# Angle casts shared between VectorE and ScalarE, longer runs of idle products, and a new searched order in a fused attention and mixer kernel

## The chip, the core and the metric

The kernel runs on one core of a Trainium2 chip. The metric is the device time of one execution in microseconds (us). Executions of one kernel mostly lie within 1 to 2.5 us of each other here, so medians are quoted with their ranges. The runs after the first comparison were made in three sessions, each on another chip, and each session timed the kernel before again (medians 358.45, 358.45 and 358.40). A ratio is the mean time of one kernel's fast runs over that of the other's fast runs of the same rounds, so it is not quite the ratio of the medians that stand beside it. TensorE is the matrix engine, VectorE and ScalarE the two engines that empty its result memory (PSUM), GpSimd issues most loads.

## The reference, cut to what matters

```python
# attention with random features: batch 8, heads 8, 576 tokens, 64 channels, 128 features
proj = einsum('bhsd,md->bhsm', x, omega)
phi  = concatenate([cos(proj), sin(proj)], -1) / sqrt(128)        # for q and for k
kv, z = einsum('bhsm,bhsd->bhmd', k_p, v), sum(k_p, axis=2)
attn  = einsum('bhsm,bhmd->bhsd', q_p, kv) / einsum('bhsm,bhm->bhs', q_p, z)   # guarded
# mixer on x = attn with the heads side by side: (8, 576, 512)
u   = x + ((x^T @ U) @ V)^T                                        # rank 32
out = u + relu(u @ w_ch1) @ w_ch2                                  # 512 -> 2048 -> 512
```

## The kernel before

The work is cut into 1294 operations: for each of 32 head pairs (8 batches, 4 pairs each) the loads, transposes, angle products, casts, sines and cosines, the products with v, the numerator and the normalisation; for each batch the mixer's two dense layers. An angle comes out of TensorE in units of 1/65536 turn as fp32; it is cast to int32, and the low 16 bits, read as int16, are the angle modulo a turn. Sine reads them directly, cosine after a quarter turn is added.

```python
o_kc = add("kcp", "DVE", 1.14, rank, lambda _: nc.vector.tensor_copy(       # cast of the keys' angles
    i32(tt.t)[:, 1280:2304], kps.t.rearrange("p a b -> p (a b)")), ...)
...
def cang(...):  nc.vector.tensor_scalar(out=i32(cc.t)[:, 0:n], in0=tt.t[:, lo:lo+n, 0], scalar1=16384.0, op0=ALU.add)
def sin(...):   nc.scalar.activation(out=fe.t[:, 1, lo:hi], in_=tt.t[:, lo:hi, 0], func=ACT.Sin, scale=SIN_SCALE)
def cos(...):   nc.scalar.activation(out=fe.t[:, 0, lo:hi], in_=cc.t[:, 0:n, 0], func=ACT.Sin, scale=SIN_SCALE)
```

The order of the operations, the engine of those that may run on either, and the buffers are two constant tables that a search outside the kernel has found. `ORDER` is a list of operation numbers; a letter behind a number picks the first or second engine allowed. Each engine runs its own operations strictly in that order. While TensorE would wait in the first 36 us (by the kernel's own timetable), it is given products of a zero tile to keep its clock up:

```python
n = int((t - last - 0.3) / 0.1) if t < FILL else 0      # how many idle products fit before this operation
if n > 0 and f + 0.1 < last:
    fill(ps.t[b], n)                                    # n products zero x zero, 128 columns
```

Of the kernel before, what the change touches and what calls it, by code (L numbers as in the profile page):

```python
# [22 lines left out]
P = 128  # L23
# [96 lines left out]
20 22 49 0 7 21a 5 6 9 10 1 50 25 77 26a 23 27 78 29 53 28a 8 105 30 32 54b 33 31 36 3 55 57 35 37 4 51 34 174 56b  # L120
58 106 12 81 24 79 107 39 82b 201 52 175 60 2 38 59 18 61 173 16 40 62 229 63 83 64 84a 109 202 41 85 66 42b 65 88
87 90 86 67 257 69 111 68 230 19 80 89 70b 43 110a 91 44 71 11b 15 112b 72 92 114 117 108 13 113 94 116 73 93 97
95 258 96 120 115 98a 45 99 46b 119 118 176 121 74a 123 122 14 47 124 278 125 75 100 126a 101 277 48a 127 177 203
102a 339 128 179 231 76b 178b 103 180b 207 208b 205 104a 181 182 259 184 185 206b 1074 187 235 129 17 135 130b
236b 131 132b 183 186 209 138 139 212 136 188 233 189 137a 234b 145 146b 190 140a 211 1075 204 338 193 191 210 147
148a 261 192 214 163 164a 167 239 1073 262a 213 215 133 168b 159 263 281 194b 195 232 216 1076 160a 358 377 242
141 218 217 196 157 279 219 237 264a 221 238 142a 342 240 220 357 161 155 396 241 243 222b 162a 223 149 158b 464
244 134a 224 169 266 260 245 156b 150a 265 247 340 249 246 268 269 225 197 165 198b 226a 376 271 170a 361 153 199
248 482 267 250b 166a 251 154b 171 200b 273 272 151 152a 143 144a 270 252 172b 274 395 280 253 254b 282 359 328
1083 1084 283b 329 255 1085 330 275 276 332 1086 256b 341 334 284 227 463 501 285 1087b 380 1077 1078 228b 331 333  # L130
335 337 521 286 287a 343 348 350 288 336 360 1079 289b 1080 347 314 352 344a 316 349 378 351 1081b 315a 345 397
312 465 317b 304 346 313b 353 305b 310 399 362 354 311b 368 296 367 366 484 588 355 320 483 589 356 1095 379 398
297a 467 363b 364 371 466 290 607 1096 1082 1097 321b 369 502 291b 370 372 306 374 307a 365 381 373 375 318 1098
385 382b 383 386 319a 486 388 390 1099b 389 292 384 1100 627 302 1089 520 293a 387 391 303a 393 646 392 324 1088
400 325b 454 456 503 1090 1091 453 394 457 401b 458 522 455 485 322 323a 402 300 294 298 403 301b 295b 460 1092
459 468 299b 473 505 404 590 472 476 1093b 1113 475 469b 1114 713 1094 405b 1115 478 1116 477 474 479 481 410
1117a 411 413 406 407 308 412 1101 480 309a 1102 409 1103 408 487 326 461 1104 462 491 488a 492 493 495 327a 1105b
470 496 504 489 497 1107 609 471 490 523 1108 1109 494 506 1110 498 500 511 524 1111b 507b 425 426a 512 429 510
591 592 1119 515 608 1120 1112 414 1121 430b 514 516 645 1122 423 513 732 415 517 419 628 499 1123a 1106 519 424b
525 578 647 526a 420a 518 579 610 431 439 508 432a 582 416 752 440a 580 1118 584 527 451 452a 581 583 509 441 449  # L140
442a 427 445 450a 629 528 529 428a 530a 585 593 446a 600 435 436a 443 444a 447 598 715 437 599 611 714 597 605
594a 417 448a 531 601 539 540 602 532 626 1125 1126 421 630 1127 587 734 418b 541 438a 648 1128 535 586 422b 753
533 603 534 595 1129b 1131 1132 1133 1124 604 536 537 606 596 1134 1135 538 612 1143 616 617 620 618 622 621 619
623 1144 1145 613a 1146 550 772 551a 558 770 751 1147 559b 649 552 553b 562 631 624 717 632b 572 733 1136 625 563b
546 547a 635 614 839 638 858 433 716 636 637 573b 877 840 639 640 1137 615 1138 1139 1140 568 434b 771 1141 1130
736 641 642 650 569b 704 643 644 651a 703 1149 560 706 735 876 561a 633 707 705 634 708 652 755 709 548 574 544
549a 1150 710 575a 653 545a 774 554 718 724 555a 654 1151 1152 1148 576 655b 577a 556 754 723 722 725 730 660 838
1153 661 726 566 570 571b 557a 662 656 1161 711 719b 564 1162 657 727 664 665 567b 895 663 1163 773 728 659 1164
565a 1165 712 542 737 741 743 742 543a 1167 1168 720 658 859 1166 857 729 746 1142 1169 745 691 692a 666 738b 744
685 747 748 842 686a 749 1170 878 721 1171 841 693 964 695 696b 756 761 861 763 694a 683 757b 762 731 671 760 860  # L150
669 750 684b 764 739 672b 1155 1156 896 758 740 897 766 1157 699 767 681 765 670a 1158 700a 982 769 759 775 768
965 1159 682b 830 1173 697 1174 831 880 776b 698a 829 777 828 833 1175 1176 832 1160 778 687 835 834 1177 688b
1178 679 843 837 779 1001 680b 848 849 850 673 780b 1179 879 667 1172 844a 781 847 851 782 689 1154 899 789 854
690a 1180 785 675 674b 677 790 786 853 836 1002 845 846 668a 701 852 1181 1182 1183 676a 678a 702a 784 862 1197
866 867 1198 791 870 783 868 863a 855 856 869 787 871 1199 1200 826 873 872 827a 881 898 1201 963 983 885 984 888
886 874 788 808 967 1191 864 882b 1003 1192 1193 1194 889 890 891 887 893 812 806 809a 865 1195 900 875 813a 807b
1196 892 894 810 955 954 824 1215 1216 953 825a 957 883 966 901b 956 960 902 804 811a 884 805a 1202 814 815a 818
903 904 905a 819a 794 959 1217 985 906 907 795a 958 1218 822 968 1219 972 975 823a 969b 816 973 1203 817b 986 1204
820 910 1205 1005 908 976 961 1206 977 974 978 911 1220 909 798 821a 987 1207 1184 1185 799b 979 993 1004 796 797a
994 802 988a 962 991 792 1186 800 980 803a 1187 913 914 912 992 1188 1189 995 981 915 793a 970 801a 996 971 943  # L160
1209 997 1210 1211 1212 998 944a 1000 1213 1006 1007a 1011 1010 1014 1012 949 1013 950a 1221 1222 919 989 920b 947
917 990 999 918b 923 1016 1015 1008 948a 1017 1020 929 924b 1214 1018 916 933 1019 1190 1208 1021a 1022 1009 1023
939 934a 921 930a 940b 1223 1024 1224 1225 1226 937 1025b 1030 1031 1033 927 922a 1026 938b 945 1027 1034 1233 931
1234 946a 925 1235 926a 928b 1236 1237 941 942a 935 1032 936a 932b 1227 1228 1029 1028 1229 1230 1238 1059 1035
1055 1060b 1037 1231 1065 1036 1066b 1056a 1039 1038a 1251 1252 1253 1254 1255 951 952b 1061 1040b 1257 1258 1047
1051 1048a 1259 1071 1052a 1072a 1260 1062b 1256 1261 1045 1067 1239 1068a 1053 1054b 1046a 1240 1063 1049 1050a
1241 1232 1041 1269 1064b 1270 1271 1272 1042b 1242 1043 1243 1273 1262 1069 1245 1057 1244 1070b 1274 1044b 1246
1247 1248 1058a 1249 1263 1281 1282 1275 1264 1250 1265 1266 1267 1268 1276 1277 1278 1279 1283 1284 1280 1287
1288 1289 1285 1286 1290 1291 1292 1293
"""  # L170
SLOTS = """
001012000103011100001411023251001002010000110112113100010103021102010001020120001013002021101312001221000000201101
020131110010214512211101010200200102113011010012201200100110100011020210111101231030240100102221213011100122210013
011225103010001002101002010102121111202210120130200211021210120031121003010122000011001110103002031010212001200211
011004123101311002021250001201203011001320012102111011023200031002102011001001210100100101321001011201312102022001
211100201001301221001021000003100021100200401101021012102100001321112511030020112001100001221011002121013210021120
013211001032002101001011020220110011100201100102010123011010013211011021100012020100021101200011020130111012010213
12201100001320102010100220210221100100110111202110101200120020201112002010200001000122021201012021002
"""

LAT = {"PE": 0.21, "DVE": 0.14, "ACT": 0.16, "POOL": 0.2, "SP": 0.15}


class Plan:
    def __init__(self):
        self.ops = []

        self.rings, self.hw, self.landed = 0.0, 0.0, []

    def add(self, *a, **k):  # L190
        o = Op(*a, **k)
        self.ops.append(o)
        return o
# [170 lines left out]
    def emit(self, order, at, nc, fill, ps):  # L364
        left, free = {}, {}
        for o in order:
            for u in o.uses:
                left[u] = left.get(u, 0) + 1
        last = 1.2
        for o, t in zip(order, at):  # L370
            for u in o.uses:
                if u.t is None:
# [20 lines left out]
def kernel(  # L393
# [145 lines left out]
    def attention(g):  # L539
# [114 lines left out]
        def i32(t):  # L654
            return t.rearrange("p a c -> p (a c)").bitcast(I32)
# [377 lines left out]
```

## Time and profile before

| | before |
|---|---|
| time, first three executions | 358.57 us median (357.65 to 359.02) |
| TensorE busy | 346.0 us of 356.5, 4136 products, 90 of them idle ones |
| VectorE, ScalarE, GpSimd busy | 258.2, 211.3, 87.9 us |
| first sine on ScalarE starts | 8.22 us |
| numerator of head pair 3 (product 405) starts | 29.10 us |
| from there to the start of the last product | 322.57 us |

The last three rows split the span in the two pieces that the prediction works with. In that split "the head" is all before the numerator of the fourth head pair of batch 0, and "the dense part" all from it on. Of the groups of instructions, the large cast is the one that the change moves (columns: line, engine, operation, tiles, shapes, count, then busy us and mean ns, then idle time before it):

```profile
L657 DVE CAST tt<-pp 128x1024 int32<-128x1024 f32 x32 | 39.0, 1219 | 7.3 <-PE pp L620 7.1
```

These are the second five transposes of head pair 3, which need its q load (called q3 below):

```profile
17.83 0.45 PE L596 MATMUL pb<-ident,qk 128*128 128x128 bf16 x5
```

There is no bracket behind it: TensorE did not wait for q3, which the trace shows landing at 12.80 or 13.49 us (two q loads follow each other there).

### The profile page before, as it was taken

The page shows a single profiled execution, that of the slowest core. Times are in us where ns is not written, and L with a number is a line of the kernel's source. Part 1 is how long each engine was busy: PE and PEld are TensorE (multiplying, and loading weights), DVE is VectorE, ACT ScalarE, POOL GpSimd, SP SyncE. Part 2 cuts the span into 40 slices and gives each one's busy share as a digit, 9 for nine tenths or more (in the row PEclk, how much of TensorE's full clock was granted, in tenths as well). Part 3 has the DMA queues.
Part 4 walks back from the last instruction along what each step waited for, and adds up shares of the span by engine and source line. Part 5 has one row for each costly group of instructions (what it writes and reads, how often), then busy time and mean ns, then how long its engine had stood idle before and what let it go on. Part 6 is the DMA issues. An engine that isn't in the chain of part 4 may idle for free.

```text
span 356.5 us, 9601 instructions
## 1 busy us (share of the span) xinstructions
PE 346.0 (97%) x4136; PEld 190.9 (54%) x4136; DVE 258.2 (72%) x422; ACT 211.3 (59%) x274; POOL 87.9 (25%) x147
## 2 busy tenths in 40 slices
PE   7879999999999999999999999999999999999994
PEld 5666566555556454555545654665445644455442
DVE  4999997797988778698768989778876853232411
ACT  3998998869575778265575674875746722121000
POOL 8884635442231435041201313001000000000000
PEclk9999999999999999999999999999999999999999
DMA  8999999999949899799747729708320415021223
GB/s 137 179 193 208 173 199 153 146 167 150 131 79 128 146 146 132 116 167 100 109 83 152 119 48 168 123 8 121 71 49 2 98 32 95 0 61 31 60 60 88
DMA packets 67403, 39.45 MB, mean 111 GB/s; under 512 B 47264, under 2 KB 61600, under 8 KB 67360
## 3 DMA queue, kind: packets, MB, share of 16 engines
q0 software_dynamic: 17376, 18.36, 37.0%
q1 hardware_dynamic: 49904, 20.34, 34.1%
q8 instruction: 32, 0.52, 0.6%
q10 hardware_dynamic: 80, 0.13, 0.1%
q14 instruction: 11, 0.09, 0.1%
HBM read 37.11 MB, written 9.44 MB: 131 GB/s over the span
## 4 chain that ended last, share of the span: by engine, by line
PE 93%; ACT 5%; DMA 1%; issue 0%; DVE 0%; POOLq 0%
PE pb L919 35%; PE pb L865 31%; PE pp L705 5%; PE pb L884 4%; PE pp L720 4%; PE pp L620 2%; ACT f L689 2%; ACT f L686 2%; PE pp L832 2%; PE pb L634 1%; PE pb L596 1%; DMA qk<-in_q_dram 1%; PE pp L726 1%; PE pb L791 1%; PE pb L996 1%; PE pb L924 1%
## 5 line engine op out<-in xcount | busy, mean ns | idle before, releaser
L865 PE MATMUL pb<-uT,W1b 128*128 128x512 bf16 x512 | 123.2, 379 | 0.0
L919 PE MATMUL pb<-W2b,hid 128*128 128x512 bf16 x512 | 122.0, 379 | 0.0
L689 ACT ACTIVATE f<-cc 128x1152 bf16<-128x1152 int16 (+1 forms) x64 | 74.3, 1162 | 21.2 <-DVE cc L682 19.7
L812 ACT ACTIVATE hid<-pb 128x512 bf16<-128x512 f32 x81 | 47.6, 597 | 64.1 <-PE pb L865 64.0
L686 ACT ACTIVATE f<-tt 128x1152 bf16<-128x1152 int16 (+1 forms) x64 | 74.4, 1162 | 9.9 <-PE pp L726 3.4
L919 PEld LDWEIGHTS <-hid 128*128 128x128 bf16 x512 | 48.1, 98 | 56.0 <-issue 3.1
L865 PEld LDWEIGHTS <-W1b 128*128 128x128 bf16 x512 | 47.5, 98 | 55.7 <-issue 3.0
L682 DVE TENSOR_SCALAR cc<-tt 128x1152 int32<-128x1152 int16 (+1 forms) x64 | 52.2, 816 | 1.2
L953 DVE TENSOR_TENSOR o<-pb,x 128x512 f32<-128x512 f32 x24 | 16.5, 689 | 44.6 <-PE pb L919 44.1
L584 POOL COPY v<-vraw 128x576 bf16<-128x576 bf16 x32 | 24.0, 751 | 92.9 <-PE pp L705 49.5
L657 DVE CAST tt<-pp 128x1024 int32<-128x1024 f32 x32 | 39.0, 1219 | 7.3 <-PE pp L620 7.1
L810 DVE TENSOR_SCALAR hid<-pb 128x512 bf16<-128x512 f32 x47 | 31.8, 684 | 13.4 <-PE pb L865 13.2
L666 DVE CAST tt<-pb 128x512 int32<-128x512 f32 x48 | 32.1, 682 | 2.1 <-PE pb L634 1.9
L555 POOL DMA_DIRECT2D qk<-in_q_dram x32 | 19.6, 620 | 31.3 <-DMA qkt<-qk 20.9
L735 DVE TENSOR_TENSOR x<-pp,rc 128x640 bf16<-128x640 f32 x32 | 26.4, 825 | 1.1
L705 PEld LDWEIGHTS <-f 64*128 64x128 bf16 x1152 | 19.6, 94 | 10.7 <-issue 6.4
L705 PE MATMUL pp<-v,f 64*128 64x65 bf16 x1152 | 23.2, 190 | 0.9 <-ACT f L689 0.9
L837 DVE TENSOR_TENSOR x<-pp,x 128x1024 bf16<-128x1024 f32 (+1 forms) x18 | 18.7, 1043 | 6.9 <-PE pp L832 6.6
L555 POOL DMA_DIRECT2D qk<-in_k_dram x31 | 18.4, 595 | 20.3 <-DMA qkt<-qk 16.2
L720 PEld LDWEIGHTS <-f 128*128 128x128 bf16 x512 | 19.9, 98 | 5.7 <-ACT f L689 0.3
L720 PE MATMUL pp<-kvb,f 128*128 128x65 bf16 x512 | 21.4, 194 | 0.1
L583 POOL DMA_DIRECT2D vraw<-in_v_dram x32 | 18.8, 591 | 3.8 <-issue 2.4
(80 smaller groups left out, 300.9 us busy)
## 6 DMA issues: line engine op xcount, KB each, us to landing
out_dram<-o SPq DMA_DIRECT2D x71, 128.0 KB, 2.5
qk<-in_q_dram POOLq DMA_DIRECT2D x32, 144.0 KB, 5.7
vraw<-in_v_dram POOLq DMA_DIRECT2D x32, 144.0 KB, 6.0
qk<-in_k_dram POOLq DMA_DIRECT2D x31, 144.0 KB, 5.8
W1b<-in_moe_w_ch_dram POOLq DMA_DIRECT2D x2, 1024.0 KB, 12.9
W2b<-in_moe_w_ch_dram POOLq DMA_DIRECT2D x4, 512.0 KB, 11.1
uT<-x SPq DMA_TRANSPOSE x30, 2.6
qkt<-qk SPq DMA_TRANSPOSE x24, 6.4
```

The lines of the kernel that those rows point to most:

```text
L555: nc.gpsimd.dma_start(qk.t[:, lo:lo + NJ, :], src[b, 2 * hp:2 * hp + 2].rearrange("h (p j) d -> (h p) j d", j=NJ))
L657: o_kc = add("kcp", "DVE", 1.14, rank, lambda _: nc.vector.tensor_copy(i32(tt.t)[:, 1280:2304], kps.t.rearrange("p a b -> p (a b)")), deps ...
L666: nc.vector.tensor_copy(i32(tt.t)[:, 640 * lo:640 * lo + 512], t.t)
L682: nc.vector.tensor_scalar(out=i32(cc.t)[:, 0:n], in0=tt.t[:, lo:lo + n, 0], scalar1=16384.0, scalar2=None, op0=ALU.add)
L686: nc.scalar.activation(out=fe.t[:, 1, lo:hi], in_=tt.t[:, lo:hi, 0], func=ACT.Sin, scale=SIN_SCALE)
L689: nc.scalar.activation(out=fe.t[:, 0, lo:hi], in_=cc.t[:, 0:n, 0], func=ACT.Sin, scale=SIN_SCALE)
L705: nc.tensor.matmul(kvp.t[:, hh, 65 * s:65 * s + 65], fe.t[pr, s, 1152 + P * jj:1280 + P * jj], v65.t[pr, KJ[jj], :], start=(jj == 0), stop ...
L720: nc.tensor.matmul(nps.t[:, hh, 65 * i:65 * i + 65], fe.t[:, s, c0:c0 + 128], kvb.t[:, hh, s, :], start=(s == 0), stop=(s == 1))
L810: nc.vector.tensor_scalar(out=o, in0=i, scalar1=0.0, scalar2=None, op0=ALU.max)
L812: nc.scalar.activation(out=o, in_=i, func=ACT.Relu)
L865: nc.tensor.matmul(hp_.t, w1h[:, ct, fs], uT.t[:, ct, 0:512], start=(ct == 0), stop=(ct == NCT - 1))
L919: nc.tensor.matmul(d, w, W2b[c4][:, f % 4, :], start=(f == 0), stop=(f == NFT - 1))
```

## The change

The intent is to let the search place each angle cast on either engine, to fill TensorE's holes in the head more tightly, and to use a new order found with more slack for late transfers.

```diff
-    o_om = add("om", "SP", 0.43, ..., post=1.35)
+    o_om = add("om", "SP", 0.43, ..., post=1.8)
...
-        last = 1.2
+        last = 1.0
...
-                n = int((t - last - 0.3) / 0.1) if t < FILL else 0
+                n = int((t - last - 0.15) / 0.107) if t < FILL else 0
...
+        both = ("DVE", "ACT")
-        o_kc = add("kcp", "DVE", 1.14, rank, lambda _: nc.vector.tensor_copy(
-            i32(tt.t)[:, 1280:2304], kps.t.rearrange("p a b -> p (a b)")), ...)
+        o_kc = add("kcp", both, (1.14, act(1024)), rank, lambda e: copy(
+            e, i32(tt.t)[:, 1280:2304], kps.t.rearrange("p a b -> p (a b)")), ...)
... (the same for tcp, 256 columns, and qcp, 512 or 1024 columns)
-ORDER, SLOTS = ... (1294 places)
+ORDER, SLOTS = ... (another order of the same 1294, 54 of 120 casts on ScalarE)
```

Part of the order of the loads (V is the mixer's small matrix, q3 the q load of head pair 3):

```diff
 old, loads in order:  ... k3  v1  q4  q3  V  v2  v3 ...
 new, loads in order:  ... v0  k3  k4  V  q3  v1  v2  v3 ...
```

## The prediction

> **What bounds the kernel now.** I read the page first (its shares and its chain), then the busy time by stretches, then the timeline of TensorE and of ScalarE in the first 30 us.
>
> ```profile
> PE 346.0 (97%) x4136; PEld 190.9 (54%) x4136; DVE 258.2 (72%) x422; ACT 211.3 (59%) x274; POOL 87.9 (25%) x147
> ...
> PE 93%; ACT 5%; DMA 1%; issue 0%; DVE 0%; POOLq 0%
> ```
>
> TensorE is busy for 97% of the span and is 93% of the chain that ended last; ScalarE has 5%. VectorE, whose casts the change moves, has none. A mean does not say where the last 3% lie, so I cut the span:
>
> ```profile
> 13.00:20.00 7.00, 5.97 (x164) 5.13 (x162) 6.96 (x11) 6.95 (x12) 6.17 (x11) 1.00 1.11 173
> 20.00:24.00 4.00, 2.76 (x70) 2.09 (x68) 3.90 (x8) 3.98 (x5) 3.61 (x7) 1.00 1.14 202
> 24.00:29.00 5.00, 3.62 (x83) 2.56 (x82) 4.93 (x11) 5.00 (x7) 3.40 (x6) 1.00 1.17 209
> ...
> 32.00:60.00 28.00, 28.00 (x447) 16.47 (x445) 26.43 (x42) 27.03 (x40) 14.32 (x21) 1.00 1.24 182
> 60.00:340.00 280.00, 280.00 (x3175) 149.19 (x3174) 202.73 (x325) 159.64 (x203) 49.45 (x80) 1.00 0.65 98
> ```
>
> The columns after the stretch's length are busy us of TensorE, its weight loads, VectorE, ScalarE, GpSimd. From 13 to 29 us it is the other way round from the rest: VectorE and ScalarE are full (ScalarE 15.93 of 16 us, VectorE 15.79), while TensorE has holes. From 32 us on TensorE has not one hole. The border is in TensorE's timeline:
>
> ```profile
> 28.73 0.24 PE L791 MATMUL pb<-x,Ub 128*32 128x128 bf16 x4 [0.36 <-DVE x L735]
> 28.79 0.22 PE L793 MATMUL pb<-x,Ut 128*32 128x128 bf16 x1
> 29.10 0.68 PE L720 MATMUL pp<-kvb,f 128*128 128x65 bf16 x16
> 29.62 0.29 PE L726 MATMUL pp<-kvb,f 128*128 128x65 bf16 x4
> ```
>
> L720 at 29.10 is the numerator of the fourth head pair of batch 0; it needs that pair's last cosine. Before it stand waits in brackets; after it no start is later than the columns of the matmul before it explain, but for about 95 ns at each change of tile shape. So the kernel is two pieces in series: a head to 29.10 us, paced by ScalarE and VectorE, and a dense TensorE part to the last product's start at 351.67. What does not shorten the head or the dense part's own work is worth nothing. The head's last steps on ScalarE are these:
>
> ```profile
> 12.47 0.58 ACT L806 COPY qkt<-pb 128x512 bf16<-128x512 bf16 x1 [0.49 <-PE pb L596]
> 12.95 1.27 ACT L689 ACTIVATE f<-cc 128x1280 bf16<-128x1280 int16 x1
> ...
> 26.84 1.15 ACT L686 ACTIVATE f<-tt 128x1152 bf16<-128x1152 int16 x1
> 27.89 1.15 ACT L689 ACTIVATE f<-cc 128x1152 bf16<-128x1152 int16 x1
> ```
>
> From the first sine at 8.22 to the last cosine's end at 29.04 ScalarE waits once, 0.49 us. One 1152-column sine starts 1.06 us after the last.
>
> **What the Trainium skill says.** "ScalarE: Activation LUTs", section "What ACT_TABLE_LOAD costs": an activation costs 186 ns + 0.833 ns per column, and neighbours overlap by about 93 ns. The trace agrees: 597 ns for 512 columns of L812 (the page's 613), 1162 for 1152 (1146). The same page, "Table sets: the hidden batching unit", has copy and relu in every set; the trace shows one table load of 1.28 us among sines, copies and relus, so a cast on ScalarE adds no load. "VectorE: DVE Perf Modes", section "Why PSUM operands drop a tier": fp32 from PSUM runs at one element a cycle; the 1024-column cast's 1219 ns is in line with 0.96 GHz plus overhead. "TensorE: Matmul & The Clock Gate", section "What's actually happening": half clock until about 3.4 us of sustained activity in a free-running window. The trace has 128-column products 106 ns apart up to about 12.0 us and 56 ns after it.
>
> **The change, part by part.**
>
> *Casts.* By the built programs, 54 of 120 angle casts move to ScalarE: 12 of the 32 1024-column key casts, 2 of 8 query casts of 1024, 27 of 48 of 512, and 13 of 32 tails of 256. Against them 16 `hid` relus of 512 go from ScalarE to VectorE (63 for 47), besides smaller copies. A 1024-column cast holds VectorE 1.14 us (start to start, 6.97 to 8.11); on ScalarE I estimate 0.92 (the 1024-column sines are 0.95 apart). In the dense part neither engine is the bound: VectorE loses 27 x 0.60 + 14 x 1.14 + 13 x 0.33 = 36 us there and in the head and gains about 10 of relus, and that buys nothing by itself.
>
> *The head, replayed by hand.* I took the new order of each engine and gave each instruction the start-to-start time that it has in the old trace. First, the input side. The first q load lands at 5.41 in both (it is first on its queue); TensorE transposes it in order at 5.46, five cold products and two idle ones, and the key angles start near 6.2 and end near 6.85, as before. The keys' first transposes do come 0.3 us earlier, since the cast no longer stands behind omega's, but they only wait for q then. Now ScalarE casts the keys (6.9 to 7.85) and the tail (to 8.12), instead of VectorE, and the first sine starts at 8.12 (8.22 before). From there ScalarE has:
> - batch 0's sixteen sines and cosines: 2 x 0.95 + 2 x 1.17 + 12 x 1.06 = 16.96 us, unchanged;
> - one query cast of 1024 (0.92), two tails (0.54), one kvb copy (0.26), the U casts (0.68), one hu copy (0.15): 2.55 us. The old order has there three qkt copies, two kvb, U and hu: 0.58 + 0.48 + 0.70 + 0.52 + 0.68 + 0.15 = 3.11 us, and the 0.49 us wait.
>
> Sum: 8.12 + 16.96 + 2.55 = 27.63, against 28.94 (start of the next operation in the old trace). VectorE keeps up in the replay, with 19.2 us of work from 6.05 on (7 transposed-tile copies, 5 of 8 large casts, 8 additions of a quarter turn at 0.68 to 0.88, two normalisations of 1.18, the small copies): its last addition would end at 26.2 and is needed at 26.56. So the gain is about 1.3 us, with only 0.3 us of margin on VectorE. I take back 0.3 us for waits that such a replay misses (the old order had 0.49). Head: -1.0 us.
>
> *Idle products.* There are 90 before and 90 after; only their places change: 27 in place of 19 at the start, more but shorter groups later. All lie before L720's place, where 405 products stand in both orders, and the useful ones among them have the same counts line by line. So they neither lengthen nor shorten the dense part. Could they warm the clock earlier? The first group ends near 3.87 instead of 3.0 and the hole after it shrinks from 0.9 to about 0.25 us, but TensorE still stops for q before 5.46. If that counts as idle, the warm clock comes at about 9 to 12 us as before. It would be worth up to 0.5 us if it came at 5. Mean: -0.1.
>
> *The dense part.* From product 405 on both have 3731 products of the same counts. Tile shapes change 76 times for 77: -0.1 us. The tail (4.4 us from the last product's end, fin and two stores) has the same instructions; -0.0.
>
> *Later loads.* W1's first half is now the 22nd load on its queue instead of 14th. Loads land 0.71 us apart in the old trace, a half of W1 takes 5.2 to 5.8. I estimate 28.3 us for the first half (first used near 32), 35 for the second (near 40), and 38 to 51 for the four parts of W2 (first used near 55, the last near 60). No wait, but less margin on W1 than before (24.41 for 32.28).
>
> Sum: 358.57 - 1.0 - 0.1 - 0.1 = 357.37; I say 357.3 us, 0.4% less.
>
> **Rivals.** (1) *VectorE takes the bound in the head*: with ScalarE relieved, a 0.2 us slip of several additions (they vary from 0.67 to 0.90) delays the last cosine. For it: VectorE was 15.79 of 16 us busy. Against: the new order takes two and a half large casts off it there. Then nothing is gained: 358.4. (2) *The dense part gets holes*: 16 more relus on VectorE, casts waiting behind sines on ScalarE, W1 later by 4 us. For it: from 32 to 60 us both engines are 94% and 97% busy. Against: the first W2 product comes earlier (place 823 for 896), which thins their work there. Cost 0.5 to 2 us: 358 to 359.5. (3) *The clock warms in the first 5 us*: everything before 9 us shortens, the first sine starts near 7.6: 356.6. (4) *The casts count in full*: 36 us off VectorE shorten the span by per cents. VectorE's 0% of the chain speaks against it; I give it nothing.
>
> **Range and chances.** The terms that can move are the head (-2.0 to 0) and holes (0 to +1.2); runs of before alone lie from 357.65 to 359.02. So 356.0 to 358.5 should hold it 8 times in 10. Two per cent is 7.2 us, half of the 15 us in which the head does no useful product at all, and far beyond either term: faster 0.01, same 0.98, slower 0.01.
>
> **What would show it.** Right: ScalarE's first sine near 8.1, its last cosine of batch 0 ending near 27.7, the L722 numerator at product 405 near 27.8 to 28.1, TensorE full from there on, clock warm at 9 to 12 us, the casts on ScalarE near 1.04 us each. Wrong: a bracketed TensorE wait after 30 us (rival 2), ScalarE's sines waiting for `cc` between 13 and 27 us (rival 1), 56 ns spacing before 8 us (rival 3). The prediction fails as a whole if the dense part's length from product 405 to the last product differs from 322.6 us by more than 0.5.

## The result, and the profile after

| | before | changed |
|---|---|---|
| median of the first four executions | 358.45 us (357.65 to 359.02) | 358.01 us (357.93 to 358.41) |
| ratio | | 0.9992, 95% interval 0.9971 to 1.0013 |
| head (numerator starts) | 29.10 | 28.53 |
| dense part | 322.57 | 322.79 |
| span of the trace | 356.5 | 356.2 |

The outcome is "same", inside the predicted range, 0.7 us above the predicted 357.3. Six more executions in a later session gave 357.61 (356.89 to 358.40; ratio 0.9957, interval 0.9916 to 0.9998, widened by the two slow executions of before). Without those two the means of that session differ by 0.8 us. All ten together have a median of 357.94. So there is probably a gain, of about half a microsecond, but the first comparison alone does not show it: its interval holds 1.

The page of the changed kernel, its line of busy times and its chain by engine:

```profile
PE 345.7 (97%) x4136; PEld 191.0 (54%) x4136; DVE 237.1 (67%) x398; ACT 226.3 (64%) x298; POOL 84.3 (24%) x147
...
PE 89%; ACT 2%; DMA 2%; DVE 2%; POOL 2%; issue 1%; ACTq 0%; DVEq 0%; POOLq 0%
```

VectorE lost 21.1 us of work (the counts of the prediction had about 26) and ScalarE gained 15.0; TensorE has the same. In the chain VectorE and GpSimd now appear with 2% each, and DMA has 2% instead of 1%: something in the head waited for a load. The busy times by stretches (columns as in the prediction):

```profile
13.00:20.00 7.00, 5.35 (x114) 4.50 (x106) 5.61 (x10) 5.44 (x10) 4.69 (x11) 0.76 0.97 156
...
24.00:29.00 5.00, 4.08 (x101) 3.15 (x100) 4.88 (x11) 4.95 (x7) 1.91 (x3) 1.00 1.06 180
...
32.00:60.00 28.00, 27.94 (x422) 16.33 (x420) 25.14 (x43) 25.00 (x34) 13.59 (x22) 1.00 1.23 183
60.00:340.00 280.00, 280.00 (x3205) 149.32 (x3198) 183.87 (x297) 175.84 (x233) 48.75 (x83) 1.00 0.59 99
```

From 32 us on it is the same picture as before: TensorE without a hole worth naming. But from 13 to 20 us, where ScalarE had been full (6.95 of 7 us), it is busy for 5.44, VectorE for 5.61, and the granted clock of TensorE is 0.76. TensorE's timeline tells what happened:

```profile
13.61 0.39 PE L635 MATMUL pp<-qkt,WT 64*128 64x512 bf16 x2
15.53 0.71 PE L597 MATMUL pb<-ident,qk 128*128 128x128 bf16 x5 [1.53 <-DMA qk<-in_q_dram]
16.04 0.85 PE L998 MATMUL pb<-zero 128*128 128x128 bf16 x6
16.68 1.09 PE L722 MATMUL pp<-kvb,f 128*128 128x65 bf16 x16
...
18.23 0.28 PE L627 MATMUL pp<-qkt,WT 64*128 64x128 bf16 x1
...
28.53 0.68 PE L722 MATMUL pp<-kvb,f 128*128 128x65 bf16 x16 [0.39 <-ACT f L691]
```

TensorE stood 1.53 us for q3 (L597 is the line of the transposes), and what follows runs at half clock: sixteen numerator products take 1.09 us, against 0.68 for sixteen such products at 28.53. The chain of the first 35 us, followed back, gives the load its length (start, us, what): it was issued at 7.40 and landed 8.08 us later, at 15.48.

```profile
7.40 8.08 DMA qk<-in_q_dram
```

ScalarE's timeline shows the two ends of this story:

```profile
7.07 1.07 ACT L688 ACTIVATE f<-tt 128x1024 bf16<-128x1024 int16 x1
...
18.57 0.37 ACT L808 CAST tt<-pp 128x256 int32<-128x256 f32 x1 [1.51 <-PE pp L628]
...
27.32 1.16 ACT L691 ACTIVATE f<-cc 128x1152 bf16<-128x1152 int16 x1
```

The first sine starts at 7.07, a full microsecond before the predicted 8.12. TensorE's clock was already warm at 5.1 us, and the first q load landed at 4.83, where the kernel before had it at 5.41; the runs below tell the two apart. Then ScalarE waits 1.51 us for the tail angles of head pair 2, which TensorE computed at 18.23 (L627 and L628). This wait is the only one of its kind, and it took back all of the early start and more. Two theories were open: q3's late landing costs the time whatever the clock does, or the clock's relapse after the wait costs it.

### The profile page after: what moved, and what is told of

Read it like the earlier page. It is cut to its first block, busy times and chain, and to the rows that moved or that the text cites. A ratio compares the mean times of both kernels' runs of the same rounds, so it can differ in the third digit from the quotient of the medians.

```text
span 356.2 us, 9626 instructions
## 1 busy us (share of the span) xinstructions
PE 345.7 (97%) x4136; PEld 191.0 (54%) x4136; DVE 237.1 (67%) x398; ACT 226.3 (64%) x298; POOL 84.3 (24%) x147
## 4 chain that ended last, share of the span: by engine, by line
PE 89%; ACT 2%; DMA 2%; DVE 2%; POOL 2%; issue 1%; ACTq 0%; DVEq 0%; POOLq 0%
PE pb L921 35%; PE pb L867 30%; PE pp L707 5%; PE pp L722 4%; PE pb L886 4%; DMA qk<-in_q_dram 2%; PE pp L834 2%; PE pp L621 2%; PE pb L635 1%; ACT f L691 1%; PE pp L728 1%; POOL qk L556 1%; ACT f L688 1%; DVE tt L806 1%; PE pb L793 1%
## 5 line engine op out<-in xcount | busy, mean ns | idle before, releaser
L921 PE MATMUL pb<-W2b,hid 128*128 128x512 bf16 x512 | 123.9, 379 | 0.0
L688 ACT ACTIVATE f<-tt 128x1152 bf16<-128x1152 int16 (+1 forms) x64 | 73.6, 1162 | 11.0 <-PE pp L728 8.8
L814 ACT ACTIVATE hid<-pb 128x512 bf16<-128x512 f32 x64 | 37.3, 595 | 49.0 <-PE pb L867 48.8
L812 DVE TENSOR_SCALAR hid<-pb 128x512 bf16<-128x512 f32 x64 | 43.1, 685 | 20.0 <-PE pb L867 19.6
L684 DVE TENSOR_SCALAR cc<-tt 128x1152 int32<-128x1152 int16 (+1 forms) x64 | 49.9, 789 | 5.2 <-ACT tt L808 4.2
L806 DVE CAST tt<-pp 128x1024 int32<-128x1024 f32 (+1 forms) x45 | 38.9, 878 | 10.2 <-PE pp L621 5.6
L585 POOL COPY v<-vraw 128x576 bf16<-128x576 bf16 x32 | 22.4, 706 | 87.7 <-PE pp L707 38.1
L808 ACT CAST tt<-pp 128x1024 int32<-128x1024 f32 (+1 forms) x27 | 18.8, 704 | 8.9 <-PE pp L628 4.4
L722 PEld LDWEIGHTS <-f 128*128 128x128 bf16 x512 | 20.7, 99 | 6.9 <-ACT f L691 0.5
L806 DVE CAST tt<-pb 128x512 int32<-128x512 f32 x21 | 14.4, 687 | 10.8 <-PE pb L635 10.6
L808 ACT CAST tt<-pb 128x512 int32<-128x512 f32 x27 | 15.5, 586 | 8.2 <-PE pb L635 8.0
```

Of the source, the lines that this page charges most:

```text
L722: nc.tensor.matmul(nps.t[:, hh, 65 * i:65 * i + 65], fe.t[:, s, c0:c0 + 128], kvb.t[:, hh, s, :], start=(s == 0), stop=(s == 1))
L806: nc.vector.tensor_copy(o, i)
L808: nc.scalar.copy(o, i)
L812: nc.vector.tensor_scalar(out=o, in0=i, scalar1=0.0, scalar2=None, op0=ALU.max)
L814: nc.scalar.activation(out=o, in_=i, func=ACT.Relu)
L921: nc.tensor.matmul(d, w, W2b[c4][:, f % 4, :], start=(f == 0), stop=(f == NFT - 1))
```

## The experiments

Twelve runs were made. The edits of ORDER are shown as the words that move.

**V behind q3.** The load of V took from 11.94 to 14.86, and q3 stood behind it.

```diff
-... 57 12 106 81 51 ...      (12 is V, 106 is q3)
+... 57 106 12 81 51 ...
```

> The changed kernel with one load moved: V's broadcast is issued just behind the q load of the fourth head pair (q3) instead of just ahead of it. Theory: in the changed kernel q3 landed at 15.48 us because V ahead of it took 2.92 us, TensorE stood 1.53 us for it in order, and that came back as ScalarE's one wait of 1.51 us. Then q3 should land near 12.7, both waits vanish, the numerator at product 405 start at 27.0 to 27.5 instead of 28.53, and the kernel take 356.5 to 357.0. Rival (VectorE is next in line at once): numerator within 0.3 us of 28.53, 358.0. Rival (the head does not set the end): numerator earlier, but the last product no earlier than 351.3.

Measured: 356.73 us median (356.61 to 357.33), ratio to before 0.9961 (0.9948 to 0.9975). q3 landed at 13.30, TensorE's wait and ScalarE's 1.51 us were gone, and the numerator started at 27.25. But the dense part had 323.41 us, 0.6 more than in the changed kernel. TensorE's timeline:

```profile
27.25 0.67 PE L722 MATMUL pp<-kvb,f 128*128 128x65 bf16 x16
...
32.66 1.68 PE L867 MATMUL pb<-uT,W1b 128*128 128x512 bf16 x7 [0.62 <-DMA W1b<-in_moe_w_ch_dram]
```

With the head shorter, the next load was late: the first half of W1 landed at 32.61 (30.98 in the changed kernel), and half of the gain went there.

**q3 one place later.** If q3's landing sets the head's end, delaying it must cost.

```diff
-... 57 12 106 81 51 56a 38 ...
+... 57 12 81 51 106 56a 38 ...
```

> The changed kernel with the q3 load one place later still, behind a v load. Theory (q3's landing sets the end of the head): it lands near 16.2, TensorE's wait for it grows from 1.5 to about 2.2 us, the numerator starts near 29.2 and the kernel takes about 358.7. Rival (q3 hidden by something else): numerator still at 28.5, 358.0. Two idle products fewer stand in it by the kernel's own rule (88 for 90), which neither theory cares for.

Measured: 357.22 us (356.75 to 357.81), ratio 0.9972 (0.9955 to 0.9989). It was not slower but faster, so the theory as I had put it fell. The trace is a lucky control: V took only 1.75 us this time, q3 landed at 15.46, within 0.02 us of the changed kernel's first trace, and TensorE stood for it almost as long:

```profile
15.51 0.45 PE L597 MATMUL pb<-ident,qk 128*128 128x128 bf16 x5 [1.12 <-DMA qk<-in_q_dram]
...
15.91 0.68 PE L722 MATMUL pp<-kvb,f 128*128 128x65 bf16 x16
...
16.81 0.23 PE L627 MATMUL pp<-qkt,WT 64*128 64x128 bf16 x1
```

The clock stayed warm. From the transposes to L627 it took 1.30 us instead of 2.70 (15.53 to 18.23), ScalarE did not wait at all, and the numerator started at 27.16. The same landing with a warm and with a cold clock thus differs by 1.4 us at L627, of which 0.2 are four idle products fewer on the way: with all six, warm traces take 1.52 and 1.53 us (after_again, after_steady_fill). (Two of its idle products had moved into the wait, which shortened the stand from 1.5 to 1.1 us and may be why the clock held.)

**A short and a long start.** The changed kernel with 19 idle products at the start, and the kernel before with 27.

```diff
-n = int((t - last - 0.15) / 0.107) if t < FILL else 0
+n = (19 if last == 1.0 else int((t - last - 0.15) / 0.107)) if t < FILL else 0    # changed kernel
-n = int((t - last - 0.3) / 0.1) if t < FILL else 0
+n = (27 if last == 1.2 else int((t - last - 0.3) / 0.1)) if t < FILL else 0       # kernel before
```

> The changed kernel with 19 idle products at the very start, as before, in place of 27. Theory: the early warm clock (56 ns spacing from 4.9 us on) comes from the unbroken start; with 19 there is a hole of about 1 us and the clock warms at 8 to 12 us; the first sine starts near 8.1 instead of 7.07, but the numerator stays near 28.5 and the time near 358.0, since q3's landing sets them. Rival (the clock alone makes the changed kernel's small gain): numerator 1 us later, 359.0. Rival (phase of the clock's window is luck): warm before 5.5 us with 19 too.

Measured: 357.48 us (357.05 to 358.02), ratio 0.9979 (0.9963 to 0.9996). The clock warmed at 10.3 us, as expected, and the first sine started at 7.80. The numerator did not stay at 28.5, it came at 27.78: q3's landing at 15.69 still held TensorE for 0.87 us, but with the later start ScalarE did not wait. This run also parts the two causes of the early sine. Its first q load landed at 4.78, as in the changed kernel's first trace, and its sine is 0.7 us later: that is the start and its clock. The second trace below has a late clock too, but that load at 5.35, and its sine comes another 0.3 us later: that is the load.

> The kernel before with 27 idle products at the very start in place of 19. Theory: clock warm before 5.5 us, first sine near 7.3 instead of 8.22, and since ScalarE is full from there on the numerator at product 405 starts 0.5 to 1.0 us earlier than 29.10 and the kernel takes 357.5 to 358.0. Rival (loads set the head there too): first sine earlier, numerator within 0.2 us of 29.1, 358.4. Rival (phase is luck): clock still cold until 9 to 12 us.

Measured: 357.87 us (357.14 to 357.91), ratio 0.9987 (0.9973 to 1.0001), which is not clear of noise. In its trace the clock was warm at 4.6 us, the first sine at 7.13 and the numerator at 27.86. So the longer start probably helps the old order too, in an execution where it works; but this trace is the fastest of the five executions, and its first q load landed early (4.49).

**The changed kernel again**, for a second trace.

> The changed kernel unaltered, for a second trace and five more times. Theory (in the first trace the 1.5 us stand for q3 fell into one window of the clock gate, the clock went cold from 15.5 to 18.6 us, and ScalarE's 1.51 us wait came from that): if the clock stays warm in this trace, the numerator starts near 27.3 to 27.8 though q3 again lands near 15.5, ScalarE's wait is under 0.5 us and the profiled time is about 357.2; if it goes cold, 28.5 and 358.0 as before. Rival (q3's landing alone): numerator at 28.3 or later with a warm clock too.

Measured: 357.61 us (356.89 to 358.40). This time the clock warmed only at 10.2 us and had no relapse. TensorE's and ScalarE's timelines:

```profile
15.68 0.45 PE L597 MATMUL pb<-ident,qk 128*128 128x128 bf16 x5 [0.59 <-DMA qk<-in_q_dram]
...
28.00 0.68 PE L722 MATMUL pp<-kvb,f 128*128 128x65 bf16 x16
```

```profile
8.08 1.07 ACT L688 ACTIVATE f<-tt 128x1024 bf16<-128x1024 int16 x1
...
18.04 0.36 ACT L808 CAST tt<-pp 128x256 int32<-128x256 f32 x1
```

q3 landed at 15.63, as late as ever, and cost ScalarE nothing: the tail cast that had waited 1.51 us starts here at 18.04 with no bracket, because ScalarE, one microsecond later by its first sine, comes to it only then.

**Idle products in the wait for q3.** 24 of them ahead of the five transposes.

```diff
-n = int((t - last - 0.15) / 0.107) if t < FILL else 0
+n = (24 if o is self.ops[111] else int((t - last - 0.15) / 0.107)) if t < FILL else 0
```

> The changed kernel with 24 idle products ahead of the five transposes that stand for q3 (24 x 56 ns = 1.34 us, less than the 1.53 us wait). q3 lands as late as ever. Theory (cold clock after the wait is the cost): clock warm throughout from 5 us on, TensorE's wait there under 0.4 us, numerator near 27.3 to 27.8, median 357.2. Rival (q3's landing is the cost): numerator at 28.5, 358.0. If the idle products run late they may cost up to 0.3 us.

Measured: 357.77 us (357.22 to 358.52), ratio 0.9964 (0.992 to 1.0009). Inconclusive: the clock warmed at 10.2 us in this trace, so that there was nothing for the idle products to prevent. They ran until 16.5, 0.8 us past q3's landing at 15.75. The numerator came at 28.29.

**V behind q3 and W1 earlier.** The q load of pair 4 (174) and W1's first half (18) move forward.

```diff
-... 230 52 13 80 86 ... 278 120 174 46b ... 73 99 18 118a ...
+... 230 52 13 174 18 80 86 ... 278 120 46b ... 73 99 118a ...
```

> V behind q3 as in the run above, and besides the q load of pair 4 and W1's first half issued two loads earlier, ahead of the loads of pair 8. In the run with V behind q3 the first W1 product waited 0.62 us for W1, which landed at 32.61. Theory: W1 lands near 29 to 31, that wait goes, the dense part from the numerator on is 322.6 to 322.9 us for 323.4, and the kernel takes 356.1 to 356.4. Rival (another transfer then comes late, pair 8's or v's): the dense part stays at 323.3, 356.7.

Measured: 356.56 us (356.46 to 358.25), ratio 0.994 (0.9898 to 0.9982). W1 landed at 27.02 and its wait is gone. The profiled execution was the slowest of the six (358.25): the clock warmed at 10.3 us, the numerator started at 28.05, and the dense part had 323.55 us with other short waits, one of 0.27 us for VectorE. So in this trace the rival's longer dense part came, though TensorE shows no wait for another load in it. Four executions lay at 356.5 and two at 357.6 and 358.25.

**The head's casts back on VectorE.** Two casts of 1024 columns and three of 256, in the version with V behind q3, with the idle products held at their places.

```diff
-... 32b ... 33b ... 62b ... 89b ... 117b ...
+... 32a ... 33a ... 62a ... 89a ... 117a ...
```

> V behind q3, with the five casts of the first four head pairs that the change gave to ScalarE put back on VectorE (two of 1024 columns, three of 256), the same order and the same 90 idle products at the same places. Theory (in the head the casts matter, VectorE and ScalarE being full there): VectorE has 3.3 us more work and ScalarE 2.6 less; VectorE becomes the bound, ScalarE waits for cc 1.5 to 2.5 us in sum, the numerator starts 1.0 to 2.0 us later than 27.28, and the kernel takes 357.7 to 358.7. Rival (the casts are worth nothing, the start and the loads made the gain): numerator within 0.4 us of 27.3, 356.8.

Measured: 360.12 us (359.27 to 362.77), ratio 1.004 (0.9982 to 1.0097). ScalarE then waits for the casts and for the additions, for example:

```profile
14.91 2.22 ACT L688 ACTIVATE f<-tt 128x1152 bf16<-128x1152 int16 x2 [2.02 <-DVE tt L806]
19.98 1.16 ACT L691 ACTIVATE f<-cc 128x1152 bf16<-128x1152 int16 x1 [1.52 <-DVE cc L684]
```

The direction is as expected, the cost larger: about 3.4 us by the medians (360.12 less 356.73; different sessions). The profiled execution was the slowest (362.77). Its numerator started at 33.63, over 6 us later than with V behind q3 where 1 to 2 were expected, and its clock was cold from 15.6 to 19.0 and from 22.4 to 29.3 us, so its waits are not those of the casts alone. This version keeps an order made for the other placing, so it overstates what the casts alone are worth.

**The dense part's casts back on VectorE.** The other 49 casts, the same way, with the head as it is.

```diff
-words such as 184b 186b 240b ... (49 casts of head pairs 4 to 31)
+              184a 186a 240a ...
```

> V behind q3, with the 49 casts of the other 28 head pairs that the change gave to ScalarE put back on VectorE, order and 90 idle products as they are. Theory (in the dense part the casts' engine buys nothing while neither VectorE nor ScalarE is full): VectorE is busy about 268 us for 237, ScalarE about 190 for 226, the head is as in the run with V behind q3 (numerator 27.2 to 28.1), and the dense part is 323.4 us plus 0 to 1.0 for holes where an order made for ScalarE puts several casts in a row on VectorE; 356.7 to 358.0. Rival (the casts count in full): VectorE's 31 us more give a kernel longer by several us, over 360.

Measured: 373.23 us (372.85 to 374.40), ratio 1.0411 (1.0385 to 1.0438). My expectation was wrong by 15 us. The page's busy line, and the longest waits of TensorE by cause (us in total, times, longest):

```profile
PE 348.9 (94%) x4136; PEld 190.9 (51%) x4136; DVE 266.8 (72%) x447; ACT 198.6 (53%) x249; POOL 85.5 (23%) x147
```

```profile
PE pp L722 <- DVE tt L806: 1.9, 4, 1.0
PE pb L921 <- DVE tt L806: 1.9, 2, 1.5
```

The head was untouched (numerator at 27.27), and the dense part took 339.44 us. VectorE is busy for 72% of the span here, the very share that it had in the kernel before, where TensorE did not wait for it after 29.10, and yet TensorE now waits for it all along. The work is not quite equal (266.8 us for 258.2; the span is longer too), so the amount is not ruled out. But 8.6 us more in a dense part that is 16 us longer points to where the casts stand: with a cast too many in a row on an engine that keeps its order, the product behind it waits. No run gave this placing an order of its own.

**The kernel before again.**

> The kernel before, unaltered, for a second trace. Theory (the moment at which the clock warms is luck of its window, about 5 or about 10 to 12 us, and sets the spread within one kernel): from the first sine to the numerator again 20.7 to 20.9 us, dense part 322.6; the first sine lies at 7.1 to 8.3 by the moment of the warm clock, and the numerator and the time follow it one to one. The changed kernel's order needs 19.9 us for the same stretch in every trace without a cold relapse.

Measured: 357.90 us (357.80 to 359.38). The profiled execution was the slowest. Clock warm at 12.0 us, first sine at 8.16, numerator at 29.32, dense part 323.42 with 0.7 us of short waits that the first trace did not have. From the first sine to the numerator it took 21.2 us, slightly more than expected. The late clock and first sine are those of the first trace, so what made this execution about 1 us slower (359.38) lies mostly in the dense part: the moment of the warm clock does not set the whole spread.

**A steady start.** Two versions with 29 idle products in the first group and 4 more in the wait for the first q load: the version with V behind q3 and W1 earlier, and the changed kernel with the 24 idle products in the wait for q3.

```diff
-n = int((t - last - 0.15) / 0.107) if t < FILL else 0
+n = (29 if last == 1.0 else 4 if o is self.ops[27] else int((t - last - 0.15) / 0.107)) if t < FILL else 0
```

> V behind q3 and W1 earlier, as above, with 29 idle products in the first group and 4 more in the wait for the first q load, so that TensorE has no hole above about 0.3 us before 6 us. Theory: the clock is warm by 8 us at the latest and in most executions by 5 to 6, the times lose their upper mode (v_w1_early had four at 356.5 and two at 357.6 and 358.3): median 356.5, none above 357.2. Rival (the modes have another cause): still some above 357.5. The 4 products may cost up to 0.4 us where the q load lands early.

Measured: 356.38 us (356.09 to 357.54), ratio to before 0.9943 (0.9922 to 0.9963). This is the fastest version by its median, though its lead over the two versions that it builds on (356.56 and 356.73) is not clear of noise. Its trace has the clock warm at 5.05 us, a numerator at 26.91 and a dense part of 322.65 us:

```profile
26.91 0.68 PE L722 MATMUL pp<-kvb,f 128*128 128x65 bf16 x16 [0.20 <-ACT f L691]
```

Two of six executions were still at 357.05 and 357.54, so not all of the upper mode went.

> The changed kernel with its loads as they are, the steady start and the 24 idle products in the wait for q3. Theory: warm early and no relapse, so the numerator starts at 27.0 to 27.6 and the median is 356.8 to 357.1 although q3 lands near 15.5 as in the changed kernel. Rival (q3's late landing costs by itself): numerator at 28.3 or later, 358.0.

Measured: 357.33 us (356.99 to 357.64), ratio 0.9964 (0.9944 to 0.9984). Clock warm at 5.0 us, no relapse, q3 landed at 15.83, numerator at 27.89. That lies between the two expectations, and ScalarE's timeline shows why:

```profile
17.67 0.37 ACT L808 CAST tt<-pp 128x256 int32<-128x256 f32 x1 [0.59 <-PE pp L628]
```

With an early warm clock, q3's landing does cost by itself, 0.6 us, even when the clock holds. By subtraction the relapse costs another 0.9 (1.51 less 0.59), but q3 landed 0.35 us later here. From the transposes to L627, with the same six idle products between, it takes 1.53 us here and 2.70 in the first trace. So my estimate for the first trace is 1.2 us for the cold clock and 0.3 for the landing.

**All traces side by side.** "Warm" is when 128-column products are first 56 ns apart; "first q" is the landing of the first q load; the last two columns are the stretch from the first sine to the numerator, and the dense part. The two runs that put casts back are left out.

| trace | warm | first q | first sine | q3 landed | numerator | sine to numerator | dense |
|---|---|---|---|---|---|---|---|
| before | 12.0 | 5.41 | 8.22 | no wait | 29.10 | 20.9 | 322.57 |
| before_again | 12.0 | 5.35 | 8.16 | no wait | 29.32 | 21.2 | 323.42 |
| before_long_start | 4.6 | 4.49 | 7.13 | no wait | 27.86 | 20.7 | 322.60 |
| after | 5.1, cold 15.3 to 18.8 | 4.83 | 7.07 | 15.48 | 28.53 | 21.5 | 322.79 |
| after_again | 10.2 | 5.35 | 8.08 | 15.63 | 28.00 | 19.9 | 322.80 |
| after_short_start | 10.3 | 4.78 | 7.80 | 15.69 | 27.78 | 20.0 | 322.65 |
| after_fill_wait | 10.2 | 5.51 | 8.24 | 15.75 | 28.29 | 20.1 | 322.81 |
| after_steady_fill | 5.0 | 4.70 | 7.23 | 15.83 | 27.89 | 20.7 | 322.79 |
| q3_later | 6.0 | 4.50 | 7.58 | 15.46 | 27.16 | 19.6 | 323.06 |
| v_behind_q3 | 5.4 | 5.16 | 7.38 | 13.30 | 27.25 | 19.9 | 323.41 |
| v_w1_early | 10.3 | 5.39 | 8.12 | 13.81 | 28.05 | 19.9 | 323.55 |
| v_w1_steady | 5.1 | 5.01 | 7.32 | 13.29 | 26.91 | 19.6 | 322.65 |

The column before the last is the change's lasting gain: 20.7 to 21.2 us in the old order, 19.6 to 20.1 in the new one wherever neither q3 nor a relapse interferes. The new order with its casts shortens the head by about 1 us from its first sine on. The "first sine" column goes with the clock, 7.1 to 7.6 with an early warm clock and 7.8 to 8.2 with a late one, and in part with the first q load. In the changed kernel's order an early start can hardly be used: the tail cast of pair 2 is reached 10.0 us after the first sine (7.07 to 17.06 in the first trace, 8.08 to 18.04 in the second), and q3 lets its angles come out at about 17.2 to 17.7 at best.

## Why the prediction was right or wrong

**The split in head and dense part** was right. The dense part from product 405 on has 322.79 us in the changed kernel against 322.57, well inside the 0.5 us that the prediction allowed. Its own small term had the wrong sign: I took 0.1 us off for one change of tile shape fewer, and the trace has 0.2 us more, in three short waits before 40 us that the old order did not have.

**The head, replayed by hand**, was right for the execution that it described, one with a late clock and the first q load near 5.4. The second trace is that execution: first sine at 8.08 (predicted near 8.1), numerator at 28.00 (27.8 to 28.1), time 357.42 (357.3). The stretch from first sine to numerator shrank by about 1.0 us, as said. The estimate for a cast on ScalarE, 1.04 us for 1024 columns, measured 1.01. The rival that VectorE takes the bound did not come: ScalarE waited for its additions and casts 0.19 us in the second trace and 0.1 in the first.

**The term that failed is the first trace's head**: -0.6 us where the sum had -1.0 for the order and -0.1 for the idle products. Three steps of the prediction were off. The step on the input side had the first q load at 5.41 in both; it landed at 4.83, worth about 0.3 us. The step on idle products gave an early clock a mean of 0.1 us and at most 0.5; it came at 5.1 us and was worth about 0.7, so that with the load the first sine moved by 1.05 us. The clock is rival (3). The step on later loads listed W1 and W2 only. It did not look at q3, which V had been put ahead of, and V is no ordinary load: it took 2.92 us there where its neighbours take about 0.72. So the early start ran into q3 at 15.48, TensorE stood 1.53 us, the clock fell, and ScalarE waited 1.51 us. The early start's microsecond was given back in one wait. That q3's landing and the relapse both take part is seen in three traces: same landing with a warm clock, no wait (q3_later, first sine 0.5 us later); warm clock and landing at 15.83, 0.59 us (after_steady_fill); cold clock, 1.51 us (after).

This accounts for the profiled execution, not for the median. The record gives each execution's mean granted clock, which leaves out the time before the first change (it is 1.000 for the kernel before, cold to 12.0 us). A relapse of 3.4 us takes 0.005 off it, as the profiled execution has (0.995, 357.95 us). The other three stood at 0.998 to 1.000 and so had no relapse, and took 357.93, 358.08 and 358.41. They have no trace, and what made them miss 357.3 stays open. That q3's load has a part in it is likely, since with V behind q3 all five executions took 356.61 to 357.33; the second trace shows that the same kernel can reach 357.42 without a relapse.

**W1 and W2** landed about 3 us later than estimated (30.98 and 37.42 for W1's halves, for 28.3 and 35; the last part of W2 at 54.17 for 51), without a wait in the changed kernel. (In the old order W1's first half is the 16th load on its queue, not the 14th.) But the margin that I called smaller was used up at once in the version with V behind q3.

**The reason given for the dense part** was half right. That moving casts to ScalarE buys nothing there is what the dense part's length shows. But I argued it from shares, VectorE being 0% of the chain, and read that as slack. Putting the casts back cost 16 us at the same 72%. A share of zero showed here that the order fitted its placing, not that there was room.

**The range and chances** held; 2% was out of reach, as argued. But the range to 358.5 also holds the median of the kernel before (358.45), so no change at all would have met it: that the result lies inside says little for the mechanism, which rests on the traces.

What stays open: how much of the 1.0 us in the head is due to the choice of engine and how much to a better search, since either alone needs a new search; why the relapse hit the first trace and not q3_later's; what puts two of six executions of the fastest version at 357 and above; and what the unprofiled executions of the changed kernel waited for. In every trace the granted clock changes only at whole steps of 3.41 us from its first change, so it counts where in a step a stand falls. In the step before the fall TensorE was busy for 1.90 of 3.41 us, or 56%; in the step of q3_later that holds its stand for 2.12, or 62%, and the clock held (columns as above, the third last is the granted clock):

```profile
11.92:15.33 3.41, 1.90 (x52) 1.22 (x46) 3.41 (x6) 3.41 (x5) 1.16 (x3) 1.00 1.20 198
15.33:18.75 3.42, 3.22 (x40) 2.91 (x40) 2.03 (x6) 1.91 (x3) 3.37 (x8) 0.50 1.06 169
```

```profile
12.72:16.13 3.41, 2.12 (x55) 1.62 (x56) 3.41 (x5) 3.41 (x5) 2.08 (x4) 1.00 1.15 183
```

The busy share alone is not the rule: the step from 349.84 to 353.25 of the first trace has 54%, and the clock held after it.

## What to carry to other kernels

When one engine is full for most of the span, find the point from which it is full and look only at what moves that point; then list every transfer that the new order moves before that point, not just the big ones, and the odd loads first. In a strictly ordered schedule an engine's share of the critical chain does not tell its slack: a placing and its order are one thing, and changing one without the other cost 16 us here. And when executions of one kernel differ by as much as the change, take a second trace before explaining the first, and ask whether what the trace shows can be in the other executions too.

## What the Trainium skill lacked or had wrong

- "TensorE: Matmul & The Clock Gate", section "HAM oscillation — how this bites in real kernels", gives the rule as no idle gaps above about 3.4 us. Here the clock fell (at 15.33, back at 18.75) during a stand of 1.53 us (13.95 to 15.53) with other short holes before it, after a step of 3.41 us in which TensorE was busy 56%. A stand of 1.12 us did not bring it down. The rule is too generous for this trace; one relapse of this kind was traced, besides those of v_casts_dve_head.
- The same page, section "What's actually happening", leaves the first warm moment to the window's phase. In the nine traces that start with 27 idle products it went with the first q load: warm at 4.6 to 6.5 us where that landed by 5.16 us (six traces), at 10.2 to 10.3 where it landed at 5.35 or later (three). With 19 idle products it never came before 10 us (three traces), with 29 and 4 more it came at 5.0 both times. So a hole of 0.4 to 0.5 us before the q load may be enough to lose it. This is a correlation; no run changed that landing alone. The phase fits the nine just as well: counted in steps of 3.41 us, the moments of the first change leave a rest of 1.0 to 3.0 us in the six early traces and of 3.2, 3.3 and 0.05 in the three late ones. With 19 products two traces were late at rests of 1.4 and 1.8, so the start counts too.
- The page's remark in that section that the ramp is under 1% of a typical kernel agrees, but the difference between 5 and 10 us moves the first sine by about 0.7 us at the same landing of the first q load (7.07 and 7.80), more than the whole change gained.
- "ScalarE: Activation LUTs", section "Rules for kernel authors", sends relu and other simple operations to VectorE, with a figure for bf16. For fp32 read from PSUM the runs show the reverse: a relu of 512 columns took 597 ns on ScalarE and 684 on VectorE in the kernel before, a cast of 1024 columns 1.01 us and 1.22 in the changed one.
- Not wrong, but easily passed over: "DMA: Bandwidth & Descriptors", section "Rules for kernel authors", warns that a leading broadcast of c copies confines a transfer to at most c engines. V's load is such a one, with 4 copies, and took 1.5 to 2.9 us where loads of the same size took about 0.72. That fits, but no run here tried another form of the load.
